# Fused windowed attention and MLP on one core: one pair's values loaded and cast at an earlier place in the order

## The chip, the cores and the metric

The kernel runs on one core of one Trainium2 chip. The metric is the device time of one execution in microseconds (us). Three runs of the kernel before gave 320.05, 319.1 and 319.5 us; the median is 319.5 us.

## The reference

Attention with a symmetric window of 32 positions over 8 batches of 8 heads, 576 positions and 64 dimensions a head, followed by two matrix products with a leaky ReLU between them. All inputs and the output are float32; the kernel computes its products in bfloat16.

```
scores = scale * np.matmul(q, k.transpose(0, 1, 3, 2))
mask = np.abs(pos[:, None] - pos[None, :]) <= window          # window = 32
scores = np.where(mask, scores, -1000000000.0)
scores = scores - np.max(scores, axis=-1, keepdims=True)
attn = np.exp(scores)
attn = attn / (np.sum(attn, axis=-1, keepdims=True) + 1e-09)
attn_out = np.matmul(attn, v)
x = attn_out.transpose(0, 2, 1, 3).reshape(B * S, H * D)       # 4608 x 512
h = x @ w_in                                                    # 512 x 2048
out = np.maximum(0.01 * h, h) @ w_out                           # 2048 x 512
```

## The kernel before

**Units of work.** Heads are taken in pairs, four pairs p = 0 to 3 a batch. A chunk i of attention is one batch b, one half of the sequence (288 positions) and one pair: i = 8 b + 4 half + p. So chunks 0 to 7 are batch 0 and chunks 8 to 15 are batch 1; chunk 8 is batch 1's first chunk and pair 0, chunk 11 is pair 3. The MLP goes in groups g of 288 rows (one half of a batch): `h_tile(g, f)` is a 128-wide piece of the hidden layer (L348 on TensorE, L355 on ScalarE), and `o_tile(j)` makes 128 rows of the output from 16 matmuls (L390), one copy on ScalarE (L395) and one store (L396).

**A chunk's steps.** `score(i)` multiplies queries and keys on TensorE (L275, five matmuls), takes the exponential on ScalarE (L280) and multiplies by the mask on GpSimd (L282, tile `prob`). `weighted(i)` sums the probabilities on TensorE (L301 or L304, tile `s`), takes the reciprocal on VectorE (L309), multiplies the probabilities by the values on TensorE (L320, tile `x`, five matmuls that read `vbd`) and scales the product on VectorE (L334, into `xT`). The tiles `s` and `x` have one buffer each.

**What a chunk needs.** Queries and keys of one pair come by `load_qk` (two DMAs on SyncE's queue, L79, 288 KB each, in runs of 1536 B), are cast to bfloat16 (`cast_qk`, L197: for batch 1 the queries on VectorE and the keys on GpSimd), transposed on TensorE (L225, six for queries and six for keys), copied out of PSUM by ScalarE (L233 and L239), and the keys are put in place in `kbd` by VectorE (`place_keys`, L258). Values come by `load_v` (two DMAs on the same queue, L91, one a head, 144 KB each, in runs of 256 B) and are cast into `vbd` by `cast_v`, two instructions, one a head, here on ScalarE (L203). The weights come on GpSimd's own DMA queue, `w_in` in four pieces and then `w_out` in four pieces (L448, L452, 512 KB each as stored).

**Order.** The whole order is written out by hand: each engine executes its instructions in the order in which this program issues them. The loads of batch 1 stand at L507 to L510: all four pairs' queries and keys, and then all four pairs' values. SyncE has eight semaphores for its transfers, and the ninth issue waits until the first has landed. Batch 1's last two pairs are cast in `second_pair` (L543): the call for pair 1 issues pair 3's casts, the call for pair 3 issues its transposes, copies and placing. The calls for pairs 0 and 1 stand in the loop at L559; after that, `spend` (L592) is called at every fourth matmul of an `o_tile` (the hook at L388) and at every `h_tile`, and does what is due. The first output tile has four such calls, turns 1 to 4, ahead of its matmuls 0, 4, 8 and 12:

- turn 1: `second_pair(2)`, so pair 2's transposes
- turn 2: `score(9)`
- turn 3: nothing
- turn 4: `second_pair(3)`, so pair 3's transposes, and after it `cast_v(1, 0, on_act=True)`, the values of chunk 8

At the next call, with the second output tile, `cast_v(1, 1)` and `step()` for chunk 8 follow: `score(10)`, then sums and product of chunk 8. On GpSimd, the mask products of chunks 8 and 9 stand behind the cast of pair 3's keys, since `score(8)` (L566) is issued after `second_pair(1)`.

Of the kernel before, what the change touches and what calls it, by code (L numbers as in the profile page):

```python
# [16 lines left out]
def kernel(  # L17
# [22 lines left out]
    NPAIR = H // 2  # L40
# [27 lines left out]
    def load_qk(b, p, behind=None):  # L68

        for into, src, name in ((qf, q, "qf"), (kf, k, "kf")):
            t = fload.tile([96, 2, RUN * D], FP32, name=f"{name}{p}")
            if behind is not None:
                behind.memset(t[0:1, 0, 0:1], 0.0)
                behind = None
            heads = src[b, 2 * p:2 * p + 2]
            if b < BY_DMA:
                nc.sync.dma_start(out=t, in_=heads.rearrange("a (p c) d -> p a (c d)", c=RUN))  # L79
            else:  # L80
                nc.sync.dma_start(
                    out=t.rearrange("p a (g e) -> p a g e", g=3),
                    in_=heads.rearrange("a (g p c) d -> p a g (c d)", g=3, c=2),
                )
            into[b, p] = t

    def load_v(b, p):

        t = fload.tile([128, NB, D], FP32, name=f"vf{p}")
        for a in range(2):  # L90
            nc.sync.dma_start(  # L91
                out=t[64 * a:64 * a + 64],
                in_=v[b, 2 * p + a].rearrange("(c p) d -> p c d", p=64),
            )
        vf[b, p] = t
# [103 lines left out]
    def cast_v(b, p, on_act=False):  # L199
        for a in range(2):  # L200
            r = slice(64 * a, 64 * a + 64)
            if on_act:
                nc.scalar.activation(out=vbd[b % 2][r, p, :, r], in_=vf[b, p][r], func=AF.Copy)  # L203
            else:
                nc.gpsimd.tensor_copy(out=vbd[b % 2][r, p, :, r], in_=vf[b, p][r])  # L205
# [61 lines left out]
    def where(i):  # L267
        return i // 8, (i // 4) % 2, i % 4

    def score(i):  # L270
        b, hf, p = where(i)
        by_c = qT[b][:, p].rearrange("p (c i) -> p c i", c=2)
        for n_, blocks in enumerate(WIN[hf]):
            for blk, i0, n in blocks:
                nc.tensor.matmul(  # L275
                    ps_v[:, n_, :, i0:i0 + n], kbd[b % 2][:, p, blk],
                    by_c[:, :, hf * EVEN + i0:hf * EVEN + i0 + n], start=True, stop=True,
                )
        e = attn.tile([128, 2 * HALF], BF16, name="e")
        nc.scalar.activation(out=e, in_=ps[:, P0:P0 + 2 * HALF], func=AF.Exp, scale=scale)  # L280
        pr = prob[:, i % NPROB]
        nc.gpsimd.tensor_mul(  # L282
            pr.rearrange("p n c i -> p (n c i)"), e, mask[hf].rearrange("p n c i -> p (n c i)"),
        )
        probs[i] = [pr, None, None]
# [134 lines left out]
    def step():  # L420


        i = state["done"]
        if JOINED - 1 <= i < NC - 1:
            join(i + 1)
        if i < NC - 2:
            score(i + 2)
        weighted(i)
        place_keys()
        for b, p in qk_due.get(i, ()):  # L430
            cast_qk(b, p)
            transpose_dma(b, p)
            if 2 < b < B - 1:
                load_qk(b + 1, p)
        if 12 < i <= 12 + NPAIR:
            load_qk(3, i - 13)
        for b, p in v_due.get(i, ()):
            cast_v(b, p)
            if b + 1 < B:
                load_v(b + 1, p)  # L440
        state["done"] += 1
# [63 lines left out]
    load_w_out(1)  # L505

    for p in range(NPAIR):  # L507
        load_qk(1, p, nc.gpsimd if p == 0 else None)
    for p in range(NPAIR):
        load_v(1, p)  # L510
    next(h0)
    next(h0)
# [30 lines left out]
    def second_pair(p):  # L543
        next(second)
        next(second)
        place_keys()
        if p + 2 < NPAIR:
            cast_qk(1, p + 2, nc.vector)
            load_qk(2, p)
        if p == 1:  # L550
            load_qk(2, 2)
            load_qk(2, 3)
# [37 lines left out]
    turn = 0  # L590

    def spend(us):  # L592
        nonlocal clock, turn
        while due and due[0] <= clock + 1e-6:
            due.pop(0)
            i = state["done"]
            if i < 11:
                cast_v(1, i - 7, on_act=True)
            step()
            if 10 <= i < 14:  # L600
                load_v(2, i - 10)
        turn += 1
        if turn == 1:
            second_pair(2)
        if turn == 2:
            score(9)
        if turn == 4:
            second_pair(3)
            cast_v(1, 0, on_act=True)
        clock += us  # L610

    for us, kind, g, f in plan:
        if kind == "h":
            spend(us)
            if f != 0:
                h_tile(g, f - 1, 2) if f == 1 else h_tile(g, f)
        elif f == 0:
            o_tile(g, lambda: spend(O_US))
# [28 lines left out]
```

## Time and profile before

| | |
|---|---|
| median of 3 runs | 319.5 us (319.1 to 320.05) |
| span of the profiled execution (first to last instruction) | 318.5 us |
| TensorE busy with matmuls (PE) | 303.2 us, 95% |
| VectorE (DVE) | 218.2 us, 69% |
| GpSimd (POOL) | 191.6 us, 60% |
| ScalarE (ACT) | 182.6 us, 57% |
| granted TensorE clock | 1.000 |
| SyncE's DMA queue (q1) | 104144 packets, 44.84 MB |
| GpSimd's DMA queue (q0) | 4224 packets, 4.19 MB |

Times in the profile count from the start of the span. A timeline row has the start of a group of instructions, its duration, the engine, the line, the operation, the tiles that it writes and reads, and how many instructions it merges; in brackets stands the idle time of the engine before it and what ended that. PE is TensorE's matmuls, PEld its weight loads, SPq SyncE, which issues DMAs; on an SPq row the duration is that of the issue alone, and the transfer lands later. The profiled span and the runs' times are not the same thing: the median is 1.0 us above the span.

### The profile page before, as it was taken

How to read it: one execution, taken by the hardware profiler on the slowest of the kernel's cores; microseconds unless marked ns; L12 is line 12 of the kernel's file. 1: busy time of each engine (PE TensorE's matmuls, PEld its weight loads, DVE VectorE, ACT ScalarE, POOL GpSimd, SP SyncE). 2: the span in 40 equal slices, each digit the busy share in tenths (PEclk: the TensorE clock that was granted, in tenths of full speed). 3: DMA queues.
4: the chain of work that ended last, by engine and by line, in shares of the span. 5: the costliest groups of instructions: out<-in, count | busy, mean ns of one | idle time of the engine just before them, and what ended most of it. 6: DMA issues, size and time to landing. Idle time of an engine off the chain costs nothing.

```text
span 318.5 us, 6474 instructions
## 1 busy us (share of the span) xinstructions
PE 303.2 (95%) x2449; PEld 204.3 (64%) x2449; DVE 218.2 (69%) x259; ACT 182.6 (57%) x393; POOL 191.6 (60%) x251
## 2 busy tenths in 40 slices
PE   2679998999999999999999999999999999999996
PEld 1467774585765858576765858576665858576653
DVE  5678955869655997688755997688745988565100
ACT  7577698474652828374652828375552837464531
POOL 7798963974546866686546866586637866330000
PEclk9999999999999999999999999999999999999999
DMA  8999999997999995399735995399733430000101
GB/s 179 211 186 218 267 250 203 250 206 181 216 242 196 231 206 150 82 251 203 155 76 127 238 227 136 75 223 232 162 76 104 109 70 33 35 35 2 66 31 71
DMA packets 108400, 49.46 MB, mean 155 GB/s; under 512 B 68816, under 2 KB 103888, under 8 KB 108368
## 3 DMA queue, kind: packets, MB, share of 16 engines
q1 hardware_dynamic: 104144, 44.84, 66.8%
q0 software_dynamic: 4224, 4.19, 8.0%
q8 instruction: 19, 0.31, 0.4%
q14 instruction: 13, 0.11, 0.1%
HBM read 36.70 MB, written 9.44 MB: 145 GB/s over the span
## 4 chain that ended last, share of the span: by engine, by line
PE 89%; DMA 3%; DVE 2%; SPq 1%; POOL 1%; ACT 1%; issue 1%; DVEq 0%; ACTq 0%
PE mm L348 39%; PE mm L390 38%; PE x L320 5%; PE ps L275 4%; DMA kf<-in_k_dram 3%; PE s L301 2%; DVE r L309 2%; SPq L79 1%; POOL w_in_bf L448 1%; DVE xT L334 1%; PE tp L225 1%; PE s L304 1%; ACT vbd L203 0%; SPq L91 0%; POOL prob L282 0%
## 5 line engine op out<-in xcount | busy, mean ns | idle before, releaser
L309 DVE RECIPROCAL r<-s 128x288 f32<-128x288 f32 x64 | 125.2, 1956 | 56.5 <-PE s L301 53.3
L282 POOL TENSOR_TENSOR prob<-e,mask 128x576 bf16<-128x576 bf16 x64 | 81.5, 1274 | 87.8 <-ACT e L280 41.1
L348 PE MATMUL mm<-xT,w_in_bf 128*128 128x288 bf16 x1024 | 134.0, 286 | 0.3
L390 PE MATMUL mm<-w_out_bf,gT 128*128 128x512 bf16 (+2 forms) x592 | 130.4, 373 | 0.2 <-DMA w_out_bf<-in_moe_w_out_dram 0.2
L355 ACT ACTIVATE gT<-mm 128x288 bf16<-128x288 f32 x256 | 101.4, 412 | 24.8 <-PE mm L348 8.5
L348 PEld LDWEIGHTS <-w_in_bf 128*128 128x128 bf16 x1024 | 98.4, 98 | 24.8 <-issue 0.6
L390 PEld LDWEIGHTS <-gT 128*128 128x128 bf16 x592 | 56.3, 98 | 59.6 <-issue 0.3
L395 ACT ACTIVATE o_sb<-mm 128x512 f32<-128x512 f32 (+2 forms) x37 | 21.7, 586 | 92.0 <-PE mm L390 92.0
L280 ACT ACTIVATE e<-ps 128x576 bf16<-128x576 f32 x64 | 41.4, 648 | 9.4 <-PE ps L275 9.2
L197 POOL CAST kb<-kf 96x384 bf16<-96x384 f32 (+1 forms) x56 | 35.5, 656 | 4.6 <-DMA kf<-in_k_dram 4.6
L205 POOL CAST vbd<-vf 64x576 bf16<-64x576 f32 x50 | 34.5, 689 | 1.8 <-DMA vf<-in_v_dram 0.4
L334 DVE TENSOR_TENSOR xT<-x,r 128x288 bf16<-128x288 f32 x64 | 29.3, 458 | 8.2 <-PE x L320 1.2
L260 DVE COPY kbd<-kT 64x576 bf16<-64x576 bf16 x48 | 32.3, 672 | 0.3
L275 PE MATMUL ps<-qT,kbd 128*128 128x128 bf16 (+2 forms) x320 | 26.5, 215 | 1.8 <-DVE kbd L258 1.2
L275 PEld LDWEIGHTS <-kbd 128*128 128x128 bf16 x320 | 21.0, 100 | 10.6 <-DVE kbd L258 1.5
L320 PE MATMUL x<-prob,vbd 128*128 128x128 bf16 (+2 forms) x320 | 26.0, 213 | 1.3 <-ACT vbd L203 0.7
L197 POOL CAST qb<-qf 96x384 bf16<-96x384 f32 x48 | 24.5, 538 | 0.0
L320 PEld LDWEIGHTS <-vbd 128*128 128x128 bf16 x320 | 20.6, 99 | 3.9 <-ACT vbd L203 1.8
L292 DVE TENSOR_TENSOR both<-prob 128x288 bf16<-128x288 bf16 x52 | 19.7, 380 | 0.9
L301 PE MATMUL s<-both,ones_bd 128*128 128x288 bf16 x52 | 14.9, 286 | 0.0
L258 DVE COPY kbd<-kT 64x576 bf16<-64x576 bf16 x16 | 7.1, 444 | 8.7 <-ACT kT L239 8.6
L225 PE MATMUL tp<-ident,qb 96*128 96x96 bf16 x48 | 4.4, 243 | 6.2 <-DVE qb L197 6.2
(43 smaller groups left out, 86.6 us busy)
## 6 DMA issues: line engine op xcount, KB each, us to landing
qf<-in_q_dram SPq DMA_DIRECT2D x32, 288.0 KB, 4.5
kf<-in_k_dram SPq DMA_DIRECT2D x32, 288.0 KB, 5.0
vf<-in_v_dram SPq DMA_DIRECT2D x64, 144.0 KB, 4.2
out_dram<-o_sb SPq DMA_DIRECT2D x35, 256.0 KB, 3.6
w_in_bf<-in_moe_w_in_dram POOLq DMA_DIRECT2D x4, 512.0 KB, 8.6
w_out_bf<-in_moe_w_out_dram POOLq DMA_DIRECT2D x4, 512.0 KB, 16.8
qT<-qb SPq DMA_TRANSPOSE x24, 4.1
kT<-kb SPq DMA_TRANSPOSE x24, 3.2
```

What stands on the lines that cost most here:

```text
L197: eng.tensor_copy(out=to, in_=tok)
L205: nc.gpsimd.tensor_copy(out=vbd[b % 2][r, p, :, r], in_=vf[b, p][r])
L260: nc.vector.tensor_copy(out=to.rearrange("p n (m c) -> p n c m", c=2), in_=kT[r].rearrange("p (c n m) -> p n c m", c=2, n=NB),)
L275: nc.tensor.matmul(ps_v[:, n_, :, i0:i0 + n], kbd[b % 2][:, p, blk], by_c[:, :, hf * EVEN + i0:hf * EVEN + i0 + n], start=True, stop=True,)
L280: nc.scalar.activation(out=e, in_=ps[:, P0:P0 + 2 * HALF], func=AF.Exp, scale=scale)
L282: nc.gpsimd.tensor_mul(pr.rearrange("p n c i -> p (n c i)"), e, mask[hf].rearrange("p n c i -> p (n c i)"),)
L309: nc.vector.reciprocal(r, s)
L320: nc.tensor.matmul(x_v[:, :, i0:i0 + n], vbd[b % 2][:, p, blk, :], pr[:, n_, :, i0:i0 + n], start=(blk == parts[0][1]), stop=(blk == parts ...
L334: nc.vector.tensor_mul(place(i), x, r)
L348: nc.tensor.matmul(h[:, 0:HALF], w_in_bf[:, c, ts(f, 128)], xT[:, c, ds(g * HALF % RING, HALF)], start=(c == 0), stop=(c == DMC - 1),)
L355: nc.scalar.activation(out=gT[:, f, ds(g * HALF % RING, HALF)].rearrange("p (i c) -> p i c", c=2), in_=h[:, 0:HALF].rearrange("p (c i) -> ...
L390: nc.tensor.matmul(o[:, lo:hi], gT[:, f, ds(128 * j % RING, 128)], w_out_bf[:, f, lo:hi], start=(f == 0), stop=(f == FFC - 1),)
```

## The change

The two transfers of batch 1's first values, `load_v(1, 0)`, move ahead of the two transfers of batch 1's last queries and keys, `load_qk(1, 3)`, on SyncE. The other loads keep their order. The cast of these values on ScalarE, `cast_v(1, 0, on_act=True)`, moves from turn 4, where it stood after `second_pair(3)`, to turn 3, ahead of it and four matmuls earlier. No instruction is added or taken away, and no size changes.

```
     for p in range(NPAIR):
+        if p == NPAIR - 1:
+            load_v(1, 0)
         load_qk(1, p, nc.gpsimd if p == 0 else None)
-    for p in range(NPAIR):
+    for p in range(1, NPAIR):
         load_v(1, p)
...
         if turn == 2:
             score(9)
+        if turn == 3:
+            cast_v(1, 0, on_act=True)
         if turn == 4:
             second_pair(3)
-            cast_v(1, 0, on_act=True)
         clock += us
```

More of the change, by code (lines that the diff above doesn't have):

```diff
@@ L507 @@
     for p in range(NPAIR):
+        if p == NPAIR - 1:
+            load_v(1, 0)
         load_qk(1, p, nc.gpsimd if p == 0 else None)
-    for p in range(NPAIR):
+    for p in range(1, NPAIR):
         load_v(1, p)
@@ L606, in spend @@
             score(9)
+        if turn == 3:
+            cast_v(1, 0, on_act=True)
         if turn == 4:
             second_pair(3)
-            cast_v(1, 0, on_act=True)
         clock += us
```

## The prediction

> **What bounds the kernel now.** I read three things first: the chain that ended last (TensorE holds 89% of it), the busy time by stage, and the timeline of TensorE around the change.
>
> ```profile
> 61.00:310.00 249.00, 249.00 (x1962) 166.28 (x1961) 174.32 (x205) 135.22 (x306) 143.49 (x190) 1.00 0.68 142
> ```
>
> The columns are the stretch, its length, and the busy time of PE, PEld, DVE, ACT and POOL. From 61 us to 310 us TensorE is busy 249.00 of 249.00 us, so no wait is left there that could absorb a shift: whatever is won or lost before 61 us goes to the end one for one. The place of the change lies just before that:
>
> ```profile
> 44.60 0.42 PE L225 MATMUL tp<-ident,qb 96*128 96x96 bf16 x6
> ...
> 46.22 1.89 PE L390 MATMUL mm<-w_out_bf,gT 128*128 128x512 bf16 x8
> 47.95 0.42 PE L225 MATMUL tp<-ident,qb 96*128 96x96 bf16 x6
> 48.20 0.42 PE L225 MATMUL tp<-ident,kb 96*128 96x96 bf16 x6
> 48.84 1.02 PE L390 MATMUL mm<-w_out_bf,gT 128*128 128x512 bf16 x4 [0.22 <-DMA w_out_bf<-in_moe_w_out_dram]
> 49.70 0.40 PE L275 MATMUL ps<-qT,kbd 128*128 128x96 bf16 x5
> 49.94 0.41 PE L304 MATMUL s<-prob,ones_bd 128*128 128x288 bf16 x2
> 51.06 0.41 PE L320 MATMUL x<-prob,vbd 128*128 128x96 bf16 x5 [0.71 <-ACT vbd L203]
> ```
>
> The reader is to see two small waits: 0.22 us for the last piece of `w_out`, and 0.71 us before chunk 8's product (51.06) for the cast of its values. The second is what the moved cast can remove. Third, the keys of the last pair, on GpSimd:
>
> ```profile
> 42.22 1.17 POOL L197 CAST kb<-kf 96x768 bf16<-96x768 f32 x1 [2.07 <-DMA kf<-in_k_dram]
> 43.34 2.05 POOL L564 MEMSET vbd<- 128x1152 bf16 x2
> 45.91 0.82 POOL L197 CAST kb<-kf 96x768 bf16<-96x768 f32 x1 [0.52 <-DMA kf<-in_k_dram]
> 46.69 2.51 POOL L282 TENSOR_TENSOR prob<-e,mask 128x576 bf16<-128x576 bf16 x2
> ```
>
> Pair 2's keys are cast from 42.22 and pair 3's from 45.91, both the moment they land, after idle time that the transfer ended. Pair 3's keys have 48.20 − 46.73 = 1.5 us in hand before TensorE takes them. Fourth, the transfers from 41.2 us on, while both queues are at work, the second block being one microsecond when the values run beside `w_out`:
>
> ```profile
> q1 hardware_dynamic: 2480, 1.09, 62.9%
> q0 software_dynamic: 753, 0.74, 56.4%
> ...
> q0 software_dynamic: 156, 0.16, 93.6%
> q1 hardware_dynamic: 153, 0.04, 29.5%
> ```
>
> The first two rows (41.2 to 48.9 us) say that 753 packets of weights are still to come at 41.2 us. The last two (45.4 to 46.4 us) say how the queues share: 156 packets of one against 153 of the other, packet by packet, although a packet of values has 256 B and one of weights 1024 B. **The order on this queue is what decides the case.**
>
> **The change, part by part.**
>
> *The cast on ScalarE* (two L203 of 0.68 us each). It leaves the place after pair 3's copies, where it ended at 51.01, and stands after chunk 9's exponential, which ends at 47.13. If the values are there, chunk 8's product can follow its sums at once: a gain of 0.71 us at most in that wait. Queued behind the moved cast are pair 3's two copies (L233, L239) and the output copy (L395); the first waits now for TensorE until 48.40. The cast ends about 48.4 (below), so this costs nothing while the transposes come no earlier than now; if they did not move, the copies would slip by less than 0.1 us.
>
> *SyncE's issues.* Two issues of values (0.60 us each when nothing holds them) go ahead of two of queries and keys. These become the ninth and tenth and wait until the first and second have landed (25.84 + 6.6 = 32.4 us, 26.20 + 8.1 = 34.3), instead of going out at 28.72 and 29.16. The queue works off its transfers in order and does not reach them before some 46 us, so the later issue costs nothing; the cover is over 10 us. The other values stay behind all of these, as now.
>
> *The transfers.* Now pair 2's keys land at 28.17 + 14.0 = 42.2, pair 3's queries at 28.72 + 15.4 = 44.1, its keys at 29.16 + 16.7 = 45.9, and the first values at 32.46 + 16.6 = 49.1 and 34.36 + 15.3 = 49.7. After the change the values come straight after 42.2. They are 2 × 64 × 9 = 1152 packets and 32 of semaphores, 1184. Weights left: 753 packets at 156 a us, 4.83 us. In that time the values get 153 a us: 739 packets. The other 445 run alone, at the rate of the stretch 48.5 to 53.0 us (3018 packets in 4.5 us, 671 a us): 0.66 us. So the values land about 42.2 + 4.83 + 0.66 = 47.7. Then pair 3's queries and keys, 384 packets and 32 of semaphores, alone: in the stretch 9.6 to 13.0 us this form made 544 packets in 3.4 us, 160 a us, so 2.6 us. **Pair 3's keys land at about 50.2 instead of 45.9.** The bounds: early, the four transfers end as a group at 49.7 as now, since their work is the same in any order; late, each half of the values takes the 3.25 us that the first takes now behind the keys (45.85 to 49.1), so 48.7, and 2.6 more, 51.3. I take 50.2, from the rates that are nearest to each stretch.
>
> A page speaks for the change: the Trainium skill, "DMA: Bandwidth & Descriptors", section on the anatomy of a DMA, has the variable part of a transfer as bytes over 436 GB/s. By that the values, 0.29 MB, would hold pair 3 up by an estimated 0.7 us, less than its 1.5 us in hand, and the sum would be a gain of 0.7 us. The rows above, with weights in the way, make it 4.3. The same page, section on queues, rings and completion order, says that an engine alternates between queues by packets of typically 9 to 17 descriptors; with such packets the values would pass the weights quickly, and the gain would again be 0.7. The trace's 153 against 156 packets of 256 and 1024 B shows no such bundling.
>
> *What is late next.* The keys' cast starts 0.05 us after landing and takes 0.82 to 1.17 us (the two rows; 1.0 is the mean of all eight): it ends at K = 50.2 + 1.05 = 51.25. TensorE stands before pair 3's key transposes, in order, and everything after them waits: 0.25 for the six transposes (48.20 less 47.95), 0.86 for four matmuls (49.70 − 48.84), 0.24 each for `score(10)` and the sums, with 0.05 of hand-over: chunk 8's product at K + 1.64 = 52.9. Now it is at 51.06. **The sum is +1.83 us**, with both old waits, 0.22 and 0.71, already gone in it. With the bounds, 49.7 and 0.82 give 52.2 (+1.2), and 51.3 and 1.17 give 54.2 (+3.1).
>
> *Covers.* GpSimd's mask product of chunk 8 stands behind the late cast: K + 1.27 (half of 2.51), done 0.1 us before the sums want it (K + 1.4). Pair 3's queries land 1.3 us before the keys; their cast on VectorE (1.18) and pair 2's placing behind it (0.91) end about 51.0, ahead of `score(10)` at 52.4. Chunk 8's reciprocal stands behind pair 3's placing on VectorE: copies from ScalarE until K + 1.1, placing 0.91, reciprocal 1.96, scaling 0.46, so K + 4.5; chunk 9's product needs it and comes 54.38 − 51.06 = 3.3 after chunk 8's, at K + 4.95. Some 0.4 us are in hand; beyond that it would cost its excess.
>
> **Rivals.**
>
> 1. *The keys arrive in time and only the wait goes.* Its place is the queue behind pair 2's keys; it holds if the values cost it less than 1.8 us there, so that the product starts before 51.06 − 0.71 = 50.35. Then the time is 319.5 − 0.7 = 318.8; with the 0.22 for weights gone as well, since their queue ends earlier, 318.6. For it: the wait is real and on the chain. Against: 1184 small packets in the way, at 153 a us.
> 2. *The wait only changes its name.* The values pass faster, the keys land near 48.9, the product starts at 51.6 and the time is 320.0. For it: once some of the sixteen engines are through with the weights they run values at far above the shared rate. Against: a transfer has landed only when its slowest engine is done, and now these four are not all in before 49.7.
> 3. *VectorE becomes the bound.* The 0.4 us in hand are gone, because the keys are at the late bound or the copies out of PSUM start late; the reciprocal of chunk 8 then delays chunk 9 too: 319.5 + 3.1 + 0.4 = 323.0. For it: the late placing puts two reciprocals close together. Against: the margin, and that only a few of the pieces have to come at their longest.
>
> **How the numbers follow.** The profiled span is 318.5 and the median 319.5, 1.0 more; I add to the median. The forecast, 70%: 319.5 + 1.83 = 321.3, in its own range of 320.7 to 322.6. Rival 1: 5%, rival 2: 15%, rival 3: 10%. The range, 319.9 to 322.7, reaches into rival 2. A difference of 0.3% is 0.96 us, about what a measurement of this kernel can tell from no change. Rival 1's best is under that, so faster is left 4%, for a cause not seen here; within it 16% (rival 2 and most of rival 1); slower 80% (forecast and rival 3).
>
> **What would show it.** Right: GpSimd's cast of pair 3's keys starts near 50.2 after idle time that `kf`'s transfer ended; TensorE idles some 2 to 3 us before pair 3's transposes, released by VectorE's `qb` or GpSimd's `kb`; the 0.71 before L320 is gone; chunk 8's product starts near 52.9; the weights land before 48.8; the stretch from there to the end is as long as now. Wrong: the keys cast before 48, no idle time at L225, and an end earlier than now. If the product starts near 52.9 and the end does not move, something after 61 us had room that I do not see.

## The result, and the profile after

The changed kernel takes 322.7 us (median of 4 runs, 322.46 to 322.93) against 319.3 us before (4 runs): a ratio of 1.0107, 95% interval 1.0091 to 1.0123. It is 3.4 us slower; the forecast was slower by 1.83.

On the page of the changed kernel, the row of the granted clock (40 slices of the span of 320.8 us, tenths of full speed) is no longer all nines. Before, and then after the change:

```profile
PEclk9999999999999999999999999999999999999999
```

```profile
PEclk9999997999999999999999999999999999999999
```

The timeline of TensorE around the change, in the columns of before:

```profile
45.76 1.89 PE L390 MATMUL mm<-w_out_bf,gT 128*128 128x512 bf16 x8
48.38 0.43 PE L225 MATMUL tp<-ident,qb 96*128 96x96 bf16 x6 [0.73 <-DVE qb L197]
50.05 0.66 PE L225 MATMUL tp<-ident,kb 96*128 96x96 bf16 x6 [1.24 <-POOL kb L197]
50.51 1.91 PE L390 MATMUL mm<-w_out_bf,gT 128*128 128x512 bf16 x4
52.21 0.66 PE L275 MATMUL ps<-qT,kbd 128*128 128x96 bf16 x5
52.66 0.69 PE L304 MATMUL s<-prob,ones_bd 128*128 128x288 bf16 x2
53.15 0.57 PE L320 MATMUL x<-prob,vbd 128*128 128x96 bf16 x5
```

Both old waits are gone: nothing stands before the four matmuls of `w_out` or before chunk 8's product. In their place TensorE waits 0.73 us for pair 3's queries and 1.24 us for its keys. And then every row is longer than it was: the four matmuls from 50.51 on take 52.21 − 50.51 = 1.70 us to the next group, where they took 0.86. What ended the wait for the keys is GpSimd's cast, and before it the transfer:

```profile
49.17 0.82 POOL L197 CAST kb<-kf 96x768 bf16<-96x768 f32 x1 [5.51 <-DMA kf<-in_k_dram]
49.96 2.50 POOL L282 TENSOR_TENSOR prob<-e,mask 128x576 bf16<-128x576 bf16 x2
```

The busy times in two neighbouring stretches of the same trace (stretch, length, busy us of PE, PEld, DVE, ACT, POOL, granted clock, DMA share, GB/s) show the lower clock and what went before it:

```profile
46.66:50.08 3.42, 1.45 (x12) 0.57 (x11) 1.36 (x3) 2.02 (x4) 0.91 (x2) 1.00 1.25 190
50.08:53.49 3.41, 3.41 (x21) 2.13 (x22) 0.99 (x3) 1.66 (x3) 2.38 (x2) 0.50 0.98 215
```

TensorE was busy 1.45 of 3.42 us, 42%, and in the 3.41 us that follow, it ran at half clock. After that it is as before: from the first hidden-layer matmul of the next group (64.16 before, 66.41 after) to the end of the span is 254.3 us in the one and 254.4 in the other.

**A common scale.** The opening, up to batch 1's first load on SyncE, differs from one execution to the next by more than some of the effects sought: that load goes out at 25.84 us in the trace of before and at 24.58 in that of after, although nothing ahead of it is changed. The clock has a part in this, how large a part is open: five score matmuls at 16.02 took 0.41 us in the trace of after, while five at 16.97 still took 0.65 in that of before, although the clock's row has a nine there in both. So I count from that load. The span less its start is 292.7 before and 296.2 after: 3.5 us more, in line with the timed 3.4.

| run | us | ratio (95% interval) | span from the load | pair 3's keys cast | chunk 8's product |
|---|---|---|---|---|---|
| before | 319.3 | | 292.7 | 20.1 | 25.2 |
| changed kernel | 322.7 | 1.0107 (1.0091 to 1.0123) | 296.2 | 24.6 | 28.6 |
| before, second trace (b0) | 319.18 | 0.9992 (0.9974 to 1.0010) | 292.7 | 20.2 | 25.2 |
| loads alone (e1_loads) | 323.22 | 1.0117 (1.0087 to 1.0146) | 296.2 | 24.5 | 28.4 |
| cast alone (e2_cast, e2_look) | 320.15 | 1.0017 (1.0005 to 1.0030) | 293.5 | 20.4 | 24.6 |
| both waits filled (e3_busy) | 321.49 | 1.0060 (1.0038 to 1.0082) | 294.6 | 24.7 | 27.2 |
| first wait filled (e4_busy_q) | 322.58 | 1.0099 (1.0074 to 1.0124) | 296.3 | 24.7 | 28.6 |
| half of the values ahead (e7_half) | 322.28, one run | | 294.3 | 23.3 | 26.8 |
| cast split (e5_split) | 318.99 | 0.9991 (0.9976 to 1.0006) | 292.0 | 20.3 | 24.6 |
| pair 3 later (e6_later) | 319.81 | 1.0013 (0.9999 to 1.0028) | 293.4 | 24.3 | 23.5 |

The last two columns are starts, in us from the load. Ratios are to the kernel before, timed beside each run. Medians and ratios leave out two far slower executions, 362.25 us of the kernel before and 1319.45 us of the cast alone; the latter was the traced one, so the row of the cast alone has its last three columns from one more execution (e2_look, 320.79 us).

### The profile page after: what moved, and what is told of

Its sections match the earlier page's. It is cut to its first block, busy times and chain, and to the rows that moved or that the text cites. A ratio compares the mean times of both kernels' runs of the same rounds, so it can differ in the third digit from the quotient of the medians.

```text
span 320.8 us, 6454 instructions
## 1 busy us (share of the span) xinstructions
PE 303.1 (94%) x2429; PEld 204.4 (64%) x2449; DVE 219.6 (68%) x259; ACT 182.7 (57%) x393; POOL 191.5 (60%) x251
## 4 chain that ended last, share of the span: by engine, by line
PE 83%; DMA 6%; SPq 3%; POOL 2%; DVE 1%; issue 1%; ACT 1%; ACTq 0%; POOLq 0%; DVEq 0%
PE mm L390 37%; PE mm L348 34%; DMA kf<-in_k_dram 6%; PE x L320 4%; PE ps L275 4%; PE s L301 2%; SPq L91 2%; SPq L79 1%; DVE r L309 1%; POOL prob L282 1%; PE s L304 1%; ACT e L280 1%; PE tp L225 1%; POOL kb L197 1%; POOL w_out_bf L452 0%
## 5 line engine op out<-in xcount | busy, mean ns | idle before, releaser
L355 ACT ACTIVATE gT<-mm 128x288 bf16<-128x288 f32 x256 | 101.2, 412 | 25.0 <-PE mm L348 8.5
L197 DVE CAST qb<-qf 96x768 bf16<-96x768 f32 x7 | 9.8, 1410 | 3.7 <-DMA qf<-in_q_dram 3.6
```

What stands on the lines that cost most here:

```text
L197: eng.tensor_copy(out=to, in_=tok)
L355: nc.scalar.activation(out=gT[:, f, ds(g * HALF % RING, HALF)].rearrange("p (i c) -> p i c", c=2), in_=h[:, 0:HALF].rearrange("p (c i) -> ...
```

## The experiments

**The kernel before once more.** No edit.

> The kernel before, unchanged, once more, for a second trace of it. The changed kernel's trace has all loads of batch 1 issued 1.26 us earlier than the trace of before (24.58 against 25.84 us), in work that the change does not touch. If that is the spread of the opening from one execution to the next, this trace shows another start than 25.84, and with the loads at s the keys of pair 3 land at s + 20.0 and chunk 8's product starts near s + 25.2 or, where TensorE's own work sets it, near 50.5. If the change itself moved the opening, this trace shows 25.84 again within 0.2. Time: 319.3, ratio 1.000 within 0.002 for both.

Measured: the load at 24.72, a span of 317.4, and the same chain behind it, in a second timeline of the kernel before:

```profile
24.72 0.32 SPq L79 DMA_DIRECT2D qf<-in_q_dram  x1
```

```profile
48.03 1.02 PE L390 MATMUL mm<-w_out_bf,gT 128*128 128x512 bf16 x4 [0.52 <-DMA w_out_bf<-in_moe_w_out_dram]
48.89 0.40 PE L275 MATMUL ps<-qT,kbd 128*128 128x96 bf16 x5
49.13 0.41 PE L304 MATMUL s<-prob,ones_bd 128*128 128x288 bf16 x2
49.95 0.41 PE L320 MATMUL x<-prob,vbd 128*128 128x96 bf16 x5 [0.42 <-ACT vbd L203]
```

The product stands 25.23 after the load, 25.22 in the first trace. So the 1.1 us between the two is the opening, and the difference of the spans, 320.8 − 318.5 = 2.3, understates the change because the first trace was of an execution that opened late.

**The loads alone.** The cast goes back behind pair 3's transposes.

```
         if turn == 2:
             score(9)
-        if turn == 3:
-            cast_v(1, 0, on_act=True)
         if turn == 4:
             second_pair(3)
+            cast_v(1, 0, on_act=True)
```

> The new order of the loads alone; the cast of the first values stays at turn 4 behind pair 3's copies. Theory A (the whole loss is pair 3's keys landing some 4 us late, and what TensorE's idle time ahead of their transposes brings with it): about as the changed kernel, 322.5 to 323.2, ratio 1.010 to 1.012, since the cast ends while TensorE still waits; half clock after the transposes again. Theory B (the cast's new place on ScalarE is a part of the loss, since it holds up what is queued behind it): clearly faster than the changed kernel, 319.3 to 321.

Measured 323.22, with half clock after the key transposes: as theory A says. The order of two pairs of transfers is the whole loss. The busy times before the clock falls and while it is low:

```profile
47.70:51.11 3.41, 0.72 (x12) 0.48 (x12) 1.36 (x3) 0.65 (x1) 1.07 (x2) 1.00 1.32 193
51.11:54.53 3.42, 3.42 (x23) 2.10 (x21) 1.30 (x3) 2.95 (x5) 2.22 (x2) 0.50 1.18 219
```

The moved cast won nothing back here: at half clock TensorE reaches the product at 53.88, after the cast in its old place has ended (52.16 + 1.39 = 53.55). At full clock its place does count, as the run with half of the values ahead shows below.

**The cast alone.** The loads of before, the cast at turn 3.

```
         if turn == 3:
             cast_v(1, 0, on_act=True)
         if turn == 4:
             second_pair(3)
-            cast_v(1, 0, on_act=True)
```

> The cast's new place alone, with the loads in the order of before. The values land at 49.1 and 49.7, so ScalarE waits for them from 47.1 on, with pair 3's two copies behind. Theory A: the product of chunk 8 starts some 0.5 us earlier, but pair 3's keys are placed 2 us later, and the reciprocal behind them on VectorE frees tile s only at 54.6, so that chunk 9's sums and product lose 0.6 to 0.8: 319.6 to 320.1, ratio 1.001 to 1.003, full clock throughout. Theory B (the cast's place is the loss): 321 or more. If the wait at the product was all that counts: 318.7, ratio 0.998.

> The cast's new place alone once more, for a trace of it; the timed runs gave 320.16. Counted from batch 1's first load, so without the opening's spread, the span is 292.7 in both traces of before. Theory A (ScalarE waits for the values with pair 3's copies behind it, pair 3's keys are placed later, and VectorE's reciprocal of chunk 8 stands behind that): 293.2 to 293.5, TensorE idle less than 0.3 before chunk 8's product and some 0.5 to 0.8 before chunk 9's sums or product, released by VectorE; full clock. Rival (the idle time only moves to the product and grows there): idle over 0.7 before chunk 8's product and none before chunk 9.

Measured 320.15, slower by 0.2%; the interval does not contain a ratio of 1. The span from the load is 293.5. The timeline of TensorE in the second run:

```profile
50.19 0.41 PE L320 MATMUL x<-prob,vbd 128*128 128x96 bf16 x5 [0.24 <-ACT vbd L203]
50.44 2.75 PE L390 MATMUL mm<-w_out_bf,gT 128*128 128x512 bf16 x12
53.98 0.40 PE L275 MATMUL ps<-qT,kbd 128*128 128x96 bf16 x5 [0.79 <-ACT e L280]
```

The product comes 0.6 us earlier, and 0.79 us are lost ahead of `score(11)`: the size is that of theory A, the place is not. ScalarE, held up by the wait for the values, gives chunk 10's exponential late, and the score tile, of which there is one, is not free for the next score. VectorE, which I had named, sits just behind and costs the product of chunk 9 some 0.3 more.

**Filling TensorE's waits.** The changed kernel, with matmuls into an unused part of the score tile.

```
     def second_pair(p):
+        if p == NPAIR - 1:
+            keep_busy(ps, 0, 7)
         next(second)
+        if p == NPAIR - 1:
+            keep_busy(ps, 0, 12)
         next(second)
```

> The changed kernel with matmuls into an unused part of the score tile while TensorE waits: 7 ahead of pair 3's query transposes, 12 between them and the key transposes, 224 columns each, some 93 ns apart. Nothing that is read changes. Theory C (the idle time of 0.73 and 1.24 us lowers the granted clock to half for 3.4 us, and this is some 1.6 us of the loss): the clock stays at 1.00, the product starts about 51.6 on the changed kernel's scale instead of 53.2, time 321.0 to 321.4, ratio 1.005 to 1.007. Theory D (the lower clock in that record costs nothing of note, the stretched rows being as the profile models them, and all of the loss is the late keys): time unchanged, 322.5 to 323, ratio 1.010 to 1.012.

The timeline of TensorE with both fills:

```profile
49.40 1.32 PE L402 MATMUL ps<-mask,ones_bd 128*128 128x224 bf16 x12
50.65 0.43 PE L225 MATMUL tp<-ident,kb 96*128 96x96 bf16 x6
50.92 1.03 PE L390 MATMUL mm<-w_out_bf,gT 128*128 128x512 bf16 x4
51.78 0.40 PE L275 MATMUL ps<-qT,kbd 128*128 128x96 bf16 x5
52.02 0.41 PE L304 MATMUL s<-prob,ones_bd 128*128 128x288 bf16 x2
52.27 0.40 PE L320 MATMUL x<-prob,vbd 128*128 128x96 bf16 x5
```

The keys are as late as in the changed kernel (cast 24.7 after the load), but the clock stays full, the four matmuls take 51.78 − 50.92 = 0.86 us again, and the span from the load is 294.6: theory C. **Of the 3.5 us, 296.2 − 294.6 = 1.6 are the clock, and 294.6 − 292.7 = 1.9 the late keys.** These are differences of single traces; the timed ratios say much the same, 1.0107 − 1.0060 or 1.5 us for the clock and 0.0060 or 1.9 us for the keys, and the two ratios' intervals don't meet.

**Only the first wait filled.** The same without the 12 matmuls.

> The changed kernel with the 7 filling matmuls ahead of pair 3's query transposes alone; nothing fills the wait between query and key transposes. How much idle time lowers the clock? If a single stretch of about 1.2 us is enough, half clock after the key transposes as in the changed kernel, 322.4 to 323, ratio 1.010. If it is the sum over some 3.4 us that counts and 0.65 us less is below the limit, full clock and the time of the run with both fills, 321.3 to 321.7, ratio 1.006.

Measured 322.58, with half clock. The busy times of the stretch before the clock falls and of the one in which it is low:

```profile
47.28:50.69 3.41, 1.25 (x17) 0.85 (x15) 1.36 (x3) 1.33 (x2) 1.00 (x2) 1.00 1.31 190
50.69:54.10 3.41, 3.41 (x23) 2.10 (x22) 1.18 (x3) 1.85 (x3) 2.28 (x2) 0.50 1.03 211
```

One measure that tells the runs apart is how busy the stretch before the fall is, when it is cut at the moments at which the clock changes. In the run with both fills, the same grid of 3.41 us has this as its emptiest stretch:

```profile
46.27:49.68 3.41, 2.34 (x22) 1.52 (x20) 1.14 (x3) 1.58 (x4) 0.00 (x0) 1.00 1.24 216
```

Busy for 1.25 of 3.41 us (37%) the clock falls, for 2.34 (69%) it doesn't. With the loads alone it was 0.72 us (21%) and it fell; in the changed kernel 42%. The run with half of the values ahead, below, has no record of the clock, but its rows show it: eight filling matmuls take 1.65 us from 18.63 and 0.93 from 22.40, so full clock begins near 22.40. In the changed kernel the fall at 50.08 comes ten stretches of 3.41 us after full clock began, at 15.95. Counted in the same way from 22.40, one stretch goes from 49.70 to 53.11. TensorE is busy in it for 1.81 us (53%), and the twelve matmuls after it take 2.75 us, as at full clock. So the limit lies between 42% and 53% on these runs, as the profile counts busy time. The run with only the first wait filled doesn't settle the alternative in its expectation cleanly: it has one wait of 1.29 us before the queries and one of 0.87 before the keys, because TensorE came to the fill earlier, so a single wait of over 1.2 us is there as well as a low sum. In the run with half the values ahead a single wait of 1.24 us left the clock full, but the stretches cut it at 49.70 into 0.45 and 0.79 us. Within one stretch the longest waits are 1.24 us and more where the clock fell, and 1.07 us (both fills) and less where it stayed full. So a limit on the longest wait in a stretch fits these runs as well as one on the sum, and which of the two counts stays open.

**Half of the values ahead.** Only one of the two transfers of values goes ahead of pair 3's queries and keys; the cast as before.

```
-    def load_v(b, p):
+    def load_v(b, p, heads=(0, 1)):
 
-        t = fload.tile([128, NB, D], FP32, name=f"vf{p}")
-        for a in range(2):
+        t = vf[b, p] if heads == (1,) else fload.tile([128, NB, D], FP32, name=f"vf{p}")
+        for a in heads:
...
     for p in range(NPAIR):
+        if p == NPAIR - 1:
+            load_v(1, 0, (0,))
         load_qk(1, p, nc.gpsimd if p == 0 else None)
+    load_v(1, 0, (1,))
-    for p in range(NPAIR):
+    for p in range(1, NPAIR):
         load_v(1, p)
```

> Only one of the two transfers of the first values goes ahead of pair 3's queries and keys; the other and the cast stay as before. Packet theory (the values pass at 153 packets a us while weights are in the way, then queries and keys at 160 a us alone): on the scale of the second trace of before, with batch 1's first load issued at 24.72, pair 3's keys land at 47.7 to 48.3, 3.0 to 3.5 us later than now and so more than half of what both transfers cost (4.3). Bytes theory (what passes ahead costs its bytes at the queue's 270 GB/s): 45.4, 0.55 later. Chunk 8's product then waits for the cast behind pair 3's copies: about 51.4 instead of 49.95, time 320.9 if the clock holds, up to 322.5 if it falls to half.

GpSimd's row for pair 3's keys in this run, whose first load went out at 26.33, and then TensorE's rows behind it:

```profile
49.62 0.82 POOL L197 CAST kb<-kf 96x768 bf16<-96x768 f32 x1 [3.76 <-DMA kf<-in_k_dram]
```

```profile
50.49 0.43 PE L225 MATMUL tp<-ident,kb 96*128 96x96 bf16 x6 [1.24 <-POOL kb L197]
50.76 1.03 PE L390 MATMUL mm<-w_out_bf,gT 128*128 128x512 bf16 x4
51.62 0.40 PE L275 MATMUL ps<-qT,kbd 128*128 128x96 bf16 x5
51.86 0.41 PE L304 MATMUL s<-prob,ones_bd 128*128 128x288 bf16 x2
53.08 0.41 PE L320 MATMUL x<-prob,vbd 128*128 128x96 bf16 x5 [0.81 <-ACT vbd L203]
53.33 2.75 PE L390 MATMUL mm<-w_out_bf,gT 128*128 128x512 bf16 x12
```

That is 23.3 after the load: 3.2 later than before, where both transfers cost 4.5. The packet theory had 3.0 to 3.5, the bytes theory 0.55. The second half costs less than the first; by the prediction's sum this is because part of it passes when the weights are through, which no run shows by itself. The product waits 0.81 for the cast behind pair 3's copies, so that it starts 53.08 − 50.44 = 2.64 after the end of the keys' cast, where it took 1.67 with the cast moved and the clock full. The span from the load is 1.6 longer than before; the one time, 322.28, has the late opening in it.

**The cast split.** The kernel before, with one of the two cast instructions on GpSimd.

```
-            if on_act:
+            if on_act and (b, p, a) != (1, 0, 1):
```

> The kernel before with its loads and order; only the second half of the first values' cast goes from ScalarE to GpSimd, which is idle there from 48.2 to 52.7. It removes most of the wait at chunk 8's product (0.42 and 0.71 us in the two traces of before) without moving a transfer: product 0.4 to 0.6 earlier, 318.9 to 319.2, ratio 0.998 to 0.999; if the wait is not worth its length, 1.000.

Measured 318.99, ratio 0.9991 with an interval from 0.9976 to 1.0006, so the times don't tell it from no change. The trace has the product 0.6 us earlier and the span from the load 0.65 shorter, as expected in size:

```profile
49.00 0.40 PE L320 MATMUL x<-prob,vbd 128*128 128x96 bf16 x5 [0.48 <-ACT vbd L203]
```

The wait itself is not gone, since TensorE comes to it earlier: the weights don't hold it up in this trace.

**Pair 3 off the path.** The change's loads and cast; pair 3 is prepared later.

```
-        if i < NC - 2:
+        if i < NC - 2 and i != 9:
             score(i + 2)
...
+        if p == 0:
+            cast_qk(1, p + 2, nc.vector)
         if p + 2 < NPAIR:
-            cast_qk(1, p + 2, nc.vector)
             load_qk(2, p)
         if p == 1:
             load_qk(2, 2)
-            load_qk(2, 3)
...
         if turn == 2:
             score(9)
+            cast_qk(1, 3, nc.vector)
+            load_qk(2, 3)
...
-        if turn == 4:
+        if turn == 7:
             second_pair(3)
+        if turn == 9:
+            score(11)
```

> The change's loads and cast, with pair 3 taken off the path: its casts go behind score(9), its transposes from turn 4 to turn 7, and score(11) from step 9 to turn 9. Pair 3's keys still land 4.3 us late, but by then nothing waits for them. If the late keys and the idle time that they bring are the whole loss, the product of chunk 8 starts near 48.3 on the scale of the second trace of before (now 49.95), the clock stays full, and the kernel is faster than before by 0.7 to 1.3 us: 318.2 to 318.9, ratio 0.996 to 0.998. If something else in the change costs time, slower than before.

The product starts 23.5 after the load, 1.75 earlier than before and where I expected it, with full clock. But the kernel takes 319.81, not less than before. The timeline of TensorE has the new waits:

```profile
54.38 0.41 PE L275 MATMUL ps<-qT,kbd 128*128 128x96 bf16 x5 [0.80 <-DVE kbd L258]
...
59.87 0.41 PE L304 MATMUL s<-prob,ones_bd 128*128 128x288 bf16 x2 [0.57 <-POOL prob L282]
```

The moved `score(11)` is still too early for the keys (0.80), and its mask product too late on GpSimd (0.57); 0.5 us of transposes only changed their place, and another 0.5 is lost after the first hidden-layer matmul of the next group. Together 2.4 against 1.75. The expectation of a gain was wrong: this order takes the late keys off the way to chunk 8's product, but pays as much behind it. That another order hides them at no cost is not shown.

## Why the prediction was wrong

- **That all of a shift reaches the end** was right: 254.3 us from the next group's first matmul to the end in before, 254.4 in after.
- **The transfers.** "Pair 3's keys land at about 50.2 instead of 45.9", 4.3 later. On the common scale the cast starts at 24.6 instead of 20.1, 4.5 later. The packet count carried over: in three microseconds of the changed kernel, 40 to 43 us, 464 packets of one queue went beside 471 of the other, the values landed at 28.05 + 18.6 = 46.65, which is 47.9 on the scale of before where 47.7 was forecast, and half the packets gave what the same count says. The weights came earlier, as said: 28.63 + 17.7 = 46.3, or 47.6 on the scale of before, against 48.8. That the end of the keys' cast was met exactly is luck: it started at 25.84 + 24.59 = 50.43, 0.18 later than forecast, and took 0.82 us where 1.0 was put in.
- **The sharing of the queues.** The prediction read 153 against 156 packets in a microsecond as showing no bundles. Equal sums alone don't show that, since bundles of equal length would give them too, and then the values would not have passed any faster. Shorter stretches of the same trace do show it: in each 0.105 us from 45.61 to 45.925, the sixteen DMA engines moved 16 packets of weights and 16 of values, one of each for every engine.
- **What is late next.** "Chunk 8's product at K + 1.64" was made of durations from the trace of before, so at full clock. With the clock held, the run with both fills took 52.27 − 50.60 = 1.67 from the end of the keys' cast to the product. In the changed kernel it took 53.15 − 49.99 = 3.16. **This is the step that failed:** the term K + 1.64 measured 3.16. I had TensorE idle for 2 to 3 us there and used, for the work right behind it, prices of a TensorE that had not been idle. The term is worth 1.6 us by the fills; without it, the sum of 1.83 stands against a measured 1.9.
- The Trainium skill has this in "TensorE: Matmul & The Clock Gate", Part 1: the clock falls to half when a window of some 3.4 us was idle and is granted again after a busy one. The traces agree on the length, 3.41 us, and on the half, 0.50. They differ from the same page's practical rule (section "Why this matters for your kernels"), no idle gap over about 3 us: the longest gap was 1.24 us in the changed kernel, and a stretch that was 42% busy was enough. I had not weighed it, and by the rule's words it would not have applied; the measurement decides.
- **The cast** was rightly costed at no loss while the transposes come no earlier. Its gain, which the sum has in it as "both old waits already gone", is real at full clock (a product 1.67 after the keys' cast with the cast moved, 2.64 with it in its old place). In the changed kernel the half clock covers it: loads alone and the full change are alike.
- **VectorE's cover held.** In the changed kernel its reciprocal of chunk 8 idles 0.98 us for TensorE's sums (53.39), so rival 3, whose 323.0 is near the measured time, was not what happened. The cover held at full clock too: in the run with both fills the reciprocal stands directly behind the placing (52.81), and chunk 9's sums and product (55.34 and 55.58) still follow without a wait. The landings of rival 1 (before 47.7) and rival 2 (near 48.9) did not come: on the scale of before the cast starts at 50.4.
- **The base.** "The profiled span is 318.5 and the median 319.5, 1.0 more" read too much into one execution. In the second trace the profiled execution took 319.09 with a span of 317.4, 1.7 more; the first trace was of a late one. The forecast of the difference, 1.83, does not depend on it.

## What to carry to other kernels

Where a stall is forecast on TensorE, price the work behind the stall as well: if the stall empties enough of a stretch of 3.4 us (here 42% busy was too little, 53% enough), the next 3.4 us run at half clock, which here nearly doubled the loss. A transfer of small packets costs its packet count while another queue is at work on the same DMA engines: here the two took turns packet by packet, so moving 0.29 MB ahead of a tight transfer cost 4.5 us; count packets, not bytes, before a load is moved. And compare traces from an event ahead of the change, since the opening can differ by as much as what is sought.

## What had not been expected of the hardware

The half clock in mid-kernel lasted 3.41 us in all three kernels that had it, and it began after stretches with TensorE 21%, 37% and 42% busy; stretches of 53% and more left it full. A short series of matmuls without use (19 of them, about 1.8 us) in the wait was worth 1.6 us.

In the trace of the changed kernel, VectorE's cast of pair 2's queries took 3.18 us instead of 0.56 to 1.18; it started 0.05 us after GpSimd's cast of pair 2's keys and ended 0.4 after GpSimd's next two instructions, so it looks as if the one had held up the other. The trace of before fits this: there the cast of 1.18 us (44.62) started beside GpSimd's two memsets (43.34 + 2.05 = 45.39) and also ended 0.4 after them. No run tests it. TensorE stood idle for 0.62 us until just after the long cast ended (44.08; ScalarE's L355, which the row names, ended at 44.09), but the runs with the short cast, loads alone and first wait filled, are no faster from the load (296.2 and 296.3 against 296.2): the later wait for the keys took it up.
